# A planner's order against a written one: the first MLP's second product in a fused attention and MLP kernel

## The chip, the cores and the metric

The kernel runs on one core of one Trainium2 chip. The metric is the device time of one execution in microseconds (us), of which the median of several runs is given. The core's engines are TensorE (PE; its weight loads are listed as PEld), VectorE (DVE), ScalarE (ACT), GpSimd (POOL, hardly used here) and SyncE (SP), which issues nearly all DMA transfers here; SPq is its queue in the profile.

## The reference

```python
x = attention(q, k, v, phi)          # 8 batches, 8 heads, 576 positions, 64 wide -> 4608 tokens of 512
h = x @ w_in;   r = np.maximum(h, 0.0);   g = s * (r * r) + b
x = (g @ w_out).astype(np.float32)                        # first MLP, 512 -> 2048 -> 512
h = x @ w_in2;  r = np.maximum(h, 0.0);   g = r * r
return (g @ w_out2).astype(np.float32)                    # second MLP, the same sizes, no s and b
```

The weights come as 64-bit floats; the kernel narrows them to 32 bits itself with integer operations.

## The kernel before, in words

There are four stages. The first computes the attention, folded into the first MLP's first product (`hidden`), and stores the ReLU'd rows `r` to DRAM (`rd`). The second, the subject here, squares them and multiplies them with `w_out` into `x1d` (tiles `ya`, `yb`, `yc`). The third is the second MLP's first product (`pa`, `pb`, `pc`), the fourth its second (`qa`, `qb`, `qc`).

Each of the three products is done by Strassen's scheme in Winograd's form: two by two quadrants, seven products in place of eight. The sums of quadrants of the weights are prepared ahead (`combos`, and for `w_in2` `prepare_in`), those of the data on the way. Each fp32 operand is split in two halves for the fast matmul format: ACT copies the operand to it, DVE subtracts the copy and so makes the rest; that pair is a *cast*. Three matmuls (`split3`) then make one product.

The second stage has six blocks of 768 tokens (`NBLK1`). For each block the four quadrants `b11`, `b12`, `b22`, `b21` are loaded in two halves each (`quad`; the room of a quad is reused by a later one: `rc_room`, and the pool `z` for `b22` and `b21`), squared on ACT (`square`), and subtracted from each other on DVE (`less`). A product `e` (0 to 6) goes in four parts, each with a cast of 128x768 (`cast`, five buffers in the pool `c_p`) and 12 matmuls. A block has 28 parts, the stage 168; a part is called a slot below, numbered through. At the end of each product two `yo` operations take it out of PSUM: ACT at e 0, 1, 2, 6, DVE at 3, 4, 5. From e 3 on each sends its result to `x1d` through SP.

Beside this, `prepare_in` makes the seven weight forms of `w_in2` for the third stage, in eight units `u` of 128 columns: load two raw halves (`wt`), narrow each in four steps (one on ACT, three on DVE, `wx`), four sums on DVE (`ws`), then seven casts of 128x256 (`wc`, two buffers), each with its own store (`wid`). It is a generator: the loop of the second stage takes a step of it once, twice or not at all per part.

What sets the order: the wrapper `Written` puts each instruction behind the one written before it on the same engine as long as `Written.held` is true. That holds in the first stage, whose lists (`TABLE`) give each step a slot of its loop (256 slots of six matmuls). At its end it becomes false, and from there the tile framework's planner chooses the order on each engine from its own costs. Then `behind()` only keeps an instruction behind the last output operation on its engine. In the second stage `ready1.upto` writes everything for part g + 4 ahead of the matmuls of part g, in the order of `block_ready`. In `BEGUN` slots of the first stage the first two squares and four casts of block 0 are already done.

Near the end of the first stage the lists also load quads of block 0: `TABLE["qd"]` gives the slots 225, 227, 240 and 244 for `b11` (two halves) and `b12` (two halves). `b22` is loaded after the stage. The room of `b12`'s second half is the one that held `w_out` units 6 and 7 until their sums are made (`wo1_combos`, tiles `w` and `ws`).

Of the kernel before, what the change touches and what calls it, by code (L numbers as in the profile page):

```python
# [8 lines left out]
F32 = mybir.dt.float32  # L9
# [8 lines left out]


# [35 lines left out]
def memory_attention_then_two_relu2_mlps(  # L55
# [22 lines left out]
    nc = tc.nc  # L78
# [154 lines left out]
    def prepare_in(pool):  # L233


        def load(u, i):
            src = w_in2.rearrange("(d p) (h f) -> d p h f", p=P, h=2)[:, :, :, u * P:u * P + P]
            raw = pool.tile([P, 1, 512], I64, tag="t", name="wt")
            for d in range(2):
                sp.dma_start(raw[:, 0, d * 2 * P:d * 2 * P + 2 * P].rearrange("p (h c) -> p h c", h=2), src[2 * i + d])  # L240
            return raw

        t = load(0, 0)
        for u in range(NU):
            yield from (None,) * (3 if u == 0 else 1)
            x = wst.tile([P, 2, 512], I32, tag="x", name="wx")
            for i in range(2):
                for step, _ in enumerate(narrow(t, None, x[:, i:i + 1])):
                    if step == 0:
                        yield  # L250
                if i == 0:
                    t = load(u, 1)
                    yield from (None,) * 3
                elif u + 1 < NU:
                    t = load(u + 1, 0)
            yield
            a11, a12, a21, a22 = of_in(x.bitcast(F32))
            sums_ = wst.tile([P, 4, 2, P], F32, tag="x", name="ws")
            s1, s2, s4, s3 = [sums_[:, i] for i in range(4)]
            for out, in0, in1, op in ((s1, a21, a22, ALU.add), (s2, s1, a11, ALU.subtract),  # L260
                                      (s3, a11, a21, ALU.subtract), (s4, a12, s2, ALU.subtract)):
                with behind():
                    dve.tensor_tensor(out=out, in0=in0, in1=in1, op=op)
            yield
            for e, of in enumerate((a11, s1, s2, s4, s3, a12, a22)):
                w = pool.tile([P, 2, 2, P], F32R, tag="wc", name="wc", bufs=2)
                with behind():
                    act.copy(w[:, 0], of)
                    dve.tensor_tensor(out=w[:, 1], in0=of, in1=w[:, 0], op=ALU.subtract)
                sp.dma_start(wid[u][:, e], w.bitcast(F32))  # L270
                yield
                if e in (1, 4):
                    yield
# [362 lines left out]
    def block_ready(n):  # L636
        items = []

        def put(k, go, *args):
            items.append((k, lambda: go(*args)))  # L640

        def less(out, in0, in1):
            out, in0, in1 = [quads[x] for x in (out, in0, in1)]
            with behind():
                dve.tensor_tensor(out=out, in0=in0, in1=in1, op=ALU.subtract)

        def square(t):
            t = quads[t]
            with behind():
                act.activation(t, t, AF.Square)  # L650

        def cast(e, part, t):
            c = c_p.tile([P, UQ, 2, TP], F32R, tag="c", name="rcast")
            src = quads[t][:, part % 2 * UQ:(part % 2 + 1) * UQ]
            with behind():
                act.copy(c[:, :, 0, :], src)
                dve.tensor_tensor(out=c[:, :, 1, :], in0=src, in1=c[:, :, 0, :], op=ALU.subtract)
            cast1[n, e, part] = c

        for e in range(7):  # L660
            for half in range(2):
                b11, b12, b22, b21 = [(n, name, half) for name in ("b11", "b12", "b22", "b21")]
                if e in (0, 1, 2, 5):
                    put(None, square, (b11, b12, b22, None, None, b21)[e])
                if e in (1, 2, 6):
                    put(None, less, *{1: (b11, b12, b11), 2: (b11, b22, b11), 6: (b21, b21, b11)}[e])
                if e == 6:
                    put(None, quad, n + 1, "b12", half)
                for part in (2 * half, 2 * half + 1):
                    put(4 * e + part, cast, e, part, (b11, b11, b11, b22, b12, b21, b21)[e])  # L670
                if e == 3:
                    put(None, less, b12, b22, b12)
                    put(None, quad, *b21)
                if e == 4:
                    put(None, *((quad, n + 1, "b11", half) if n + 1 < NBLK1 else (x_first, half)))
                if e == 6:
                    put(None, quad, n + 1, "b22", half)
        return items

    ready1 = Ready(NBLK1, block_ready)  # L680


# [55 lines left out]
    for at_, (name, half) in zip(TABLE["qd"], (("b11", 0), ("b11", 1), ("b12", 0), ("b12", 1))):  # L738
        on(at_, quad, 0, name, half)
# [6 lines left out]
    for slot in range(SB * B):  # L746
        b, h = divmod(slot, SB)
        f, half = divmod(h, 2)
        if h == 0 and b == B - 2:
            kpart.close()  # L750
            wpools.append(ctx.enter_context(tc.tile_pool(name="wa", bufs=1)))
            turns.append((in_turn([wo1_combos(u) for u in range(NA)]), 1))
        for go, args in events.pop(slot, []):
            go(*args)
        if h == 0 and b == B - 1:
            lpart.close()
            wpools.append(ctx.enter_context(tc.tile_pool(name="wb", bufs=1)))
# [10 lines left out]
        if slot == BEGUN[0]:  # L768
            begun = block_ready(0)
            ready1.items = lambda n: begun if n == 0 else block_ready(n)  # L770
        for _ in range(BEGUN.count(slot)):
            begun.pop(0)[1]()
    assert not events
    Written.held = False
# [50 lines left out]

    for n in range(NBLK1):
        banks, outs = {}, {}
        if n == NBLK1 - 1:
            for _ in win:
                pass  # L830
            w64x.close()
            xpools[1] = ctx.enter_context(tc.tile_pool(name="xc0", bufs=1))
        for e in range(7):
            key = "acacaba"[e]
# [4 lines left out]
            for part in range(4):  # L839
                ahead = 28 * n + 4 * e + part + 4  # L840
                ready1.upto(ahead // 28, ahead % 28)
                for _ in range((1, 0, 1, 2, 1, 1, 1)[e]):
                    next(win, None)
                for d in range(2):
                    for u in range(UQ):
                        w = weight("one", part * UQ + u, e)
                        for i, (wi, xi) in enumerate(split3):
                            nc.tensor.matmul(to[d], lhsT=w[:, wi, d], rhs=cast1[n, e, part][:, u, xi],  # L848
                                             start=(start and part == 0 and u == 0 and i == 0),
                                             stop=(part == 3 and u == UQ - 1 and i == 2), skip_group_check=True)  # L850
            which, high = ((0, 0), (1, 1), (0, 1), (0, 1), (1, 1), (0, 0), (1, 0))[e]
            key = which, high
            if key not in outs:
                outs[key] = o1_p.tile([P, 2, TP], F32, tag="o", name="yo")
                for d in range(2):
                    st["act"] = nc.scalar.activation(outs[key][:, d], to[d], AF.Identity,
                                                     scale=s_sb[:, 0:1], bias=wsum[:, 2 * which + d:2 * which + d + 1])
            else:
                for d in range(2):
                    o = outs[key][:, d]  # L860
                    st["dve"] = nc.vector.scalar_tensor_tensor(out=o, in0=to[d], scalar=s_sb[:, 0:1], in1=o,
                                                               op0=ALU.mult, op1=ALU.add)
            if e > 2:
                t0 = n * TB + high * TP
                nc.sync.dma_start(x1d[t0 // XG][:, 2 * which:2 * which + 2, t0 % XG:t0 % XG + TP], outs[key])
# [194 lines left out]
```

## Time and profile before

| | |
|---|---|
| median of 3 runs | 1449.47 us (1446.84 to 1450.83) |
| the profiled execution | 1449.36 us, span 1447.6 us |
| mean granted clock of TensorE | 0.996 |
| PE busy | 1402.8 us, 97% of the span |
| DVE busy | 1073.6 us, 74% |
| ACT busy | 796.2 us, 55% |

All other times stand in the rows below and are microseconds from the span's start. Durations of neighbouring instructions on one engine overlap a little, so a merged row (x2, x48) is shorter than the sum of its members.

### The profile page before, as it was taken

What the parts mean: (1) busy time and instruction counts of PE and PEld (TensorE: products, weight loads), DVE (VectorE), ACT (ScalarE), POOL (GpSimd) and SP (SyncE); (2) the same over time, 40 slices, a digit from 0 to 9 for tenths busy, and PEclk for the clock granted to TensorE, in tenths of its full rate; (3) what the DMA queues carried; (4) which work ended last, traced back from release to release, by engine and by line L of the source; (5) the groups of instructions that cost most, each with busy time, mean ns of one, the idle gap of its engine ahead of it and who ended that gap; (6) DMA issues with size and microseconds to landing.
All of it is one profiled execution on the core that took longest, in us unless ns stands there. A gap on an engine that the chain in (4) does not pass through costs nothing.

```text
span 1447.6 us, 28018 instructions
## 1 busy us (share of the span) xinstructions
PE 1402.8 (97%) x11360; PEld 1347.9 (93%) x11360; DVE 1073.6 (74%) x1550; ACT 796.2 (55%) x1403; POOL 1.2 (0%) x8
## 2 busy tenths in 40 slices
PE   4899999998999999999999999999999999999998
PEld 2688888888999999999999999999999999999998
DVE  6767787666798988888758687786657776777775
ACT  3555666677767767677445455454434444444443
POOL 0000000000000000000000000000000000000000
PEclk9999999999999999999999999999999999999999
DMA  9979888536585584854895664756797334433441
GB/s 299 302 240 290 281 276 283 186 121 217 158 272 183 181 266 148 270 163 164 303 369 193 234 232 168 283 174 259 266 356 262 112 122 146 146 125 111 129 146 30
DMA packets 211473, 306.44 MB, mean 212 GB/s; under 512 B 48656, under 2 KB 163344, under 8 KB 203792
## 3 DMA queue, kind: packets, MB, share of 16 engines
q1 hardware_dynamic: 211184, 304.40, 62.8%
q8 instruction: 89, 1.46, 0.4%
q14 instruction: 40, 0.33, 0.1%
q10 hardware_dynamic: 160, 0.26, 0.0%
HBM read 180.88 MB, written 123.73 MB: 210 GB/s over the span
## 4 chain that ended last, share of the span: by engine, by line
PE 71%; DVE 11%; DMA 9%; ACT 4%; issue 3%; SPq 1%; ACTq 0%; DVEq 0%
PE qa L143 14%; PE pa L141 13%; PE hps L143 13%; PE qc L143 7%; PE pc L141 7%; PE qb L143 4%; PE ya L848 3%; PE pb L141 3%; DVE rcast L141 3%; DMA wid<-wc 3%; PE vps L143 2%; DMA r<-rd 2%; DMA wt<-in_moe_w_in_dram 2%; DVE r L141 2%; PE sp L143 1%
## 5 line engine op out<-in xcount | busy, mean ns | idle before, releaser
L143 PEld LDWEIGHTS hps<-pt,vp 128*128 128x128 f32 x1536 | 208.2, 188 | 37.6 <-issue 18.3
L143 PE MATMUL hps<-pt,vp 128*128 128x288 f32 x1536 | 233.2, 303 | 5.1 <-ACT r L143 2.3
L143 ACT CAST gc<-h 128x1024 fp32r<-128x1024 f32 x119 | 123.3, 1049 | 172.2 <-DVE h L143 171.7
L143 PE MATMUL qa<-w,gc 128*128 128x256 f32 x1728 | 216.7, 283 | 1.1 <-DVE gc L143 0.8
L143 PEld LDWEIGHTS qa<-w,gc 128*128 128x128 f32 x1728 | 211.4, 192 | 1.5 <-DVE gc L143 1.0
L848 PE MATMUL ya<-rcast,w 128*128 128x384 f32 x1152 | 206.2, 338 | 6.3 <-DVE rcast L141 3.8
L143 DVE TENSOR_TENSOR gc<-h,gc 128x1024 fp32r<-128x1024 f32 x119 | 145.6, 1224 | 87.8 <-ACT gc L143 87.7
L848 PEld LDWEIGHTS ya<-rcast,w 128*128 128x128 f32 x1152 | 201.2, 189 | 8.5 <-DVE rcast L141 5.4
L141 PE MATMUL pa<-xc,w 128*128 128x384 f32 x1104 | 204.2, 337 | 0.0
L141 PEld LDWEIGHTS pa<-xc,w 128*128 128x128 f32 x1104 | 192.9, 188 | 0.7 <-DVE gr L141 0.4
L143 ACT ACTIVATE r<-hps 128x288 f32<-128x288 f32 x256 | 104.5, 417 | 66.9 <-PE hps L143 50.1
L143 PE MATMUL qc<-w,gc 128*128 128x256 f32 x864 | 109.5, 283 | 0.0
L848 PE MATMUL yc<-rcast,w 128*128 128x384 f32 x576 | 104.6, 340 | 4.6 <-DVE rcast L141 4.0
L848 PEld LDWEIGHTS yc<-rcast,w 128*128 128x128 f32 x576 | 101.4, 191 | 6.1 <-DVE rcast L141 5.1
L143 PEld LDWEIGHTS qc<-w,gc 128*128 128x128 f32 x864 | 106.3, 192 | 0.0
L141 PE MATMUL pc<-xc,w 128*128 128x384 f32 x552 | 104.0, 336 | 0.0
L141 DVE TENSOR_TENSOR rcast<-r,rcast 128x768 fp32r<-128x768 f32 x92 | 84.3, 953 | 18.0 <-ACT rcast L141 17.9
L141 PEld LDWEIGHTS pc<-xc,w 128*128 128x128 f32 x552 | 96.6, 188 | 0.3 <-DVE xc L822 0.3
L141 ACT CAST rcast<-r 128x768 fp32r<-128x768 f32 x92 | 73.5, 832 | 12.5 <-PE ya L848 5.9
L141 ACT ACTIVATE gr<-pa 128x384 f32<-128x384 f32 x46 | 22.6, 492 | 101.1 <-PE pa L141 101.1
L141 ACT CAST rcast<-rz 128x768 fp32r<-128x768 f32 x72 | 58.7, 834 | 32.4 <-DVE rz L141 15.2
L141 DVE SCALAR_TENSOR_TENSOR gr<-gr 128x384 f32<-128x384 f32 x138 | 73.7, 553 | 1.9
(277 smaller groups left out, 1857.4 us busy)
## 6 DMA issues: line engine op xcount, KB each, us to landing
rd<-r SPq DMA_DIRECT2D x128, 288.0 KB, 4.0
gd<-gr SPq DMA_DIRECT2D x96, 384.0 KB, 3.6
h<-gd SPq DMA_DIRECT2D x34, 1024.0 KB, 5.4
wt<-in_moe_w_out_dram SPq DMA_DIRECT2D x16, 1024.0 KB, 6.8
wid<-wc SPq DMA_DIRECT2D x56, 256.0 KB, 3.8
r<-rd SPq DMA_DIRECT2D x16, 768.0 KB, 5.4
rz<-rd SPq DMA_DIRECT2D x16, 768.0 KB, 6.6
kv<-in_k_dram SPq DMA_DIRECT2D x24, 384.0 KB, 5.3
```

The lines of the kernel that those rows point to most:

```text
L141: return go(*args, **kwargs)
L143: self.last = go(*args, **kwargs)
L848: nc.tensor.matmul(to[d], lhsT=w[:, wi, d], rhs=cast1[n, e, part][:, u, xi], start=(start and part == 0 and u == 0 and i == 0), stop=(part ...
```

## The change

In the second stage `Written.held` stays true on all four engine wrappers: PE, ACT, DVE and SP. `block_steps` gives every square, subtraction, cast and load a slot, by the offsets of `BLK`; within a slot casts come first, then squares, subtractions, loads. Block 0's first eight slots have their own list (`FIRST`). `prepare_in` becomes single operations with a slot each (`WIN`, cut below): `n` is one narrowing step of a half, `s` two of the four sums, `p` a cast of a pair of forms. The casts go by pairs (128x512, the seventh alone), so there are four copies, four subtractions and five stores per unit. The pairs live in the same two tags as the raw loads (`t0`, `t1`), while before there were one buffer for raw loads and two for `wc`. The second half of `b12` of block 0 is loaded after the first stage. The pool `z` is opened ahead of `o1`. The preparation now ends in slot 152; before, what was left of it was done at the start of the last block.

```diff
+WIN = ((0, "load", 0, 0), (0, "load", 0, 1), (5, "n", 0, 0, 0), (8, "n", 0, 0, 1), (9, "n", 0, 0, 2), (9, "n", 0, 0, 3), (9, "n", 0, 1, 0), (11,
...
+       3), (90, "s", 4, 0), (90, "s", 4, 1), (91, "p", 4, 0), (92, "p", 4, 1), (95, "p", 4, 2), (96, "p", 4, 3), (97, "load", 5, 0), (98, "load",
+       5, 1), (101, "n", 5, 0, 0), (102, "n", 5, 0, 1), (102, "n", 5, 0, 2), (102, "n", 5, 0, 3), (102, "n", 5, 1, 0), (103, "n", 5, 1, 1), (103,
+       "n", 5, 1, 2), (106, "n", 5, 1, 3), (107, "s", 5, 0), (109, "s", 5, 1), (111, "p", 5, 0), (113, "p", 5, 1), (115, "p", 5, 2), (117, "load",
...
+       2), (139, "n", 7, 0, 3), (140, "n", 7, 1, 0), (141, "n", 7, 1, 1), (141, "n", 7, 1, 2), (143, "n", 7, 1, 3), (146, "s", 7, 0), (146, "s", 7,
+       1), (147, "p", 7, 0), (148, "p", 7, 1), (151, "p", 7, 2), (152, "p", 7, 3))
+BEGIN1 = (("sq", 0, "b11"), ("cast", 0, 0), ("cast", 0, 1), ("sq", 1, "b11"), ("cast", 0, 2), ("cast", 0, 3))
+FIRST = ((0, "sq", 0, "b12"), (0, "less", 0, "b11", "b12", "b11"), (0, "cast", 1, 0), (1, "cast", 1, 1), (1, "sq", 1, "b12"),
+         (1, "less", 1, "b11", "b12", "b11"), (2, "cast", 1, 2), (3, "cast", 1, 3), (3, "sq", 0, "b22"), (3, "less", 0, "b11", "b22", "b11"),
+         (4, "cast", 2, 0), (5, "cast", 2, 1), (5, "sq", 1, "b22"), (5, "less", 1, "b11", "b22", "b11"), (6, "cast", 2, 2), (7, "cast", 2, 3))
+BLK = {"sq": {0: -5, 1: -8, 2: -8, 5: -5}, "less": {1: -6, 2: -6, 4: -6, 6: -6}, "cast": -4, "b21": 10, "b11": 14, "b12": 18, "b22": 22}
...
+        def pair(u, k):
+            x = xs[u].bitcast(F32).rearrange("p i f -> p (i f)").rearrange("p (e k h c) -> p h e k c", e=2, k=2, h=2)
+            of = (ts["s", u][:, 0:2], ts["s", u][:, 2:4], x[:, 0], x[:, 1, 1:2])[k]
+            m = 2 if k < 3 else 1
+            w = pool.tile([P, 2, 2, 2, P], F32R, tag=f"t{k % 2}", name="wc")[:, :m]
+            act.copy(w[:, :, 0], of)
+            dve.tensor_tensor(out=w[:, :, 1], in0=of, in1=w[:, :, 0], op=ALU.subtract)
+            for i in range(1) if k != 2 else range(2):
+                e, j = ((1, slice(0, 2)), (3, slice(0, 2)), (5 * i, slice(i, i + 1)), (6, slice(0, 1)))[k]
+                sp.dma_start(wid[u][:, e:e + (2 if k < 2 else 1)], w[:, j].bitcast(F32))
...
+        for n in range(NBLK1):
+            for e in range(7):
+                g = 28 * n + 4 * e
+                for half in range(2):
+                    h = 2 * half
+                    name = {0: "b11", 1: "b12", 2: "b22", 5: "b21"}.get(e)
+                    if name and g + h + BLK["sq"][e] >= 0:
+                        on(g + h + BLK["sq"][e], 2, square, n, half, name)
...
+                    for part in (h, h + 1):
+                        if g + part + BLK["cast"] >= 0:
+                            on(g + part + BLK["cast"], 1, cast, n, e, part)
...
-    for at_, (name, half) in zip(TABLE["qd"], (("b11", 0), ("b11", 1), ("b12", 0), ("b12", 1))):
+    for at_, (name, half) in zip(TABLE["qd"], (("b11", 0), ("b11", 1), ("b12", 0))):
...
-    Written.held = False
...
+    z_pool.append(bpart.enter_context(tc.tile_pool(name="z", bufs=1, side="right")))
     o1_p = bpart.enter_context(tc.tile_pool(name="o1", bufs=3, side="right"))
-    z_pool.append(bpart.enter_context(tc.tile_pool(name="z", bufs=1, side="right")))
...
-    for half in range(2):
-        quad(0, "b22", half)
+    for name, half in (("b12", 1), ("b22", 0), ("b22", 1)):
+        quad(0, name, half)
...
             for part in range(4):
-                ahead = 28 * n + 4 * e + part + 4
-                ready1.upto(ahead // 28, ahead % 28)
-                for _ in range((1, 0, 1, 2, 1, 1, 1)[e]):
-                    next(win, None)
+                for go, *args in parts.pop(28 * n + 4 * e + part, []) + win.pop(28 * n + 4 * e + part, []):
+                    go(*args)
...
+    assert not parts
+    Written.held = False
```

## Rows read from the trace of the kernel before

**Rows 1.** Waits of PE, second stage: waiter, releaser, us in total, times, longest.

```profile
PE yc L848 <- DVE rcast L141: 4.0, 4, 1.9
PE ya L848 <- DVE rcast L141: 3.8, 4, 1.6
...
PE yc L848 <- ACT rcast L141: 0.6, 1, 0.6
PE ya L848 <- ACT rcast L141: 0.2, 1, 0.2
```

**Rows 2.** Timeline, PE: start, duration, what, count, idle before it and releaser.

```profile
362.72 10.17 PE L848 MATMUL ya<-rcast,w 128*128 128x384 f32 x48 [2.28 <-ACT r L143]
...
598.47 7.74 PE L848 MATMUL ya<-rcast,w 128*128 128x384 f32 x43 [1.58 <-DVE rcast L141]
...
718.81 8.48 PE L848 MATMUL ya<-rcast,w 128*128 128x384 f32 x48
...
727.13 2.27 PE L141 MATMUL pa<-xc,w 128*128 128x384 f32 x12
...
1079.08 3.04 PE L143 MATMUL qa<-w,gc 128*128 128x256 f32 x24
```

**Rows 3.** Windows: stretch, length, engines' busy us, granted clock, DMA share, GB/s.

```profile
363.60:367.00 3.40, 3.40 (x13) 3.40 (x12) 2.93 (x2) 2.95 (x4) 0.00 (x0) 0.50 0.29 114
...
554.80:558.10 3.30, 3.30 (x12) 3.30 (x11) 2.98 (x4) 3.30 (x4) 0.00 (x0) 0.50 0.39 146
...
483.40:544.00 60.60, 59.89 (x344) 59.26 (x344) 52.99 (x70) 41.21 (x55) 0.00 (x0) 1.00 0.64 206
```

**Rows 4.** Timeline, one stall: ACT's hold and PE's wait after it.

```profile
544.71 0.41 ACT L141 CAST wc<-ws 128x256 fp32r<-128x256 f32 x1 [4.88 <-DMA wid<-wc]
...
553.43 6.88 PE L848 MATMUL yc<-rcast,w 128*128 128x384 f32 x29 [1.86 <-DVE rcast L141]
```

**Rows 5.** Timeline of SP's queue and of ACT where the second stage starts.

```profile
347.29 3.63 SPq L143 DMA_DIRECT2D rd<-r  x2
356.22 0.92 SPq L143 DMA_DIRECT2D r<-rd  x2
357.20 5.82 SPq L143 DMA_DIRECT2D rd<-r  x6
...
359.71 0.88 ACT L143 CAST rcast<-r 128x768 fp32r<-128x768 f32 x1
361.96 0.71 ACT L143 ACTIVATE r<-hps 128x288 f32<-128x288 f32 x2 [1.37 <-DMA rd<-r]
362.55 2.87 ACT L141 ACTIVATE r<-r 128x1536 f32<-128x1536 f32 x2
```

**Rows 6.** Waits of SP's queue from 340 to 375 us.

```profile
SPq L143 <- DVE w L143: 5.2, 1, 5.2
```

**Rows 7.** Groups by line and shape, second stage: busy us, mean ns of one.

```profile
L141 DVE TENSOR_TENSOR rcast<-r,rcast 128x768 fp32r<-128x768 f32 x92 | 84.3, 953 | 18.0 <-ACT rcast L141 17.9
L141 ACT CAST rcast<-r 128x768 fp32r<-128x768 f32 x92 | 73.5, 832 | 12.5 <-PE ya L848 5.9 <-DVE r L141 5.6
...
L141 DVE TENSOR_TENSOR r<-rz,r 128x1536 f32<-128x1536 f32 x24 | 41.6, 1753 | 4.4 <-ACT rz L141 4.4
...
L141 DVE SCALAR_TENSOR_TENSOR wx<-wt,wx 128x512 int32<-128x512 int32 x32 | 22.0, 687 | 0.4
...
L141 DVE TENSOR_TENSOR wc<-ws,wc 128x256 fp32r<-128x256 f32 x32 | 13.4, 420 | 13.9 <-ACT wc L141 13.7
...
L861 DVE SCALAR_TENSOR_TENSOR yo<-yc,s_sb,yo 128x384 f32<-128x384 f32 x12 | 7.2, 611 | 0.0
```

**Rows 8.** DMA issues from 350 to 727 us: count, KB each, median us to landing.

```profile
wid<-wc SPq DMA_DIRECT2D x56, 256.0 KB, 3.8
...
r<-rd SPq DMA_DIRECT2D x14, 384.0 KB, 4.8
```

More of the change, by code (lines that the diff above doesn't have):

```diff
@@ L233, in prepare_in @@
     def prepare_in(pool):
+        ts, xs, steps = {}, {}, {}
         def load(u, i):
             src = w_in2.rearrange("(d p) (h f) -> d p h f", p=P, h=2)[:, :, :, u * P:u * P + P]
-            raw = pool.tile([P, 1, 512], I64, tag="t", name="wt")
+            ts[u, i] = pool.tile([P, 1, 512], I64, tag=f"t{i}", name="wt")
             for d in range(2):
-                sp.dma_start(raw[:, 0, d * 2 * P:d * 2 * P + 2 * P].rearrange("p (h c) -> p h c", h=2), src[2 * i + d])
-            return raw
@@ L243, in prepare_in @@
[L243 to L250, printed above, removed]
-                if i == 0:
[L252 to L273, printed above, removed]
@@ L275, in load_out @@
+        for at_, go, *args in WIN:
+            steps.setdefault(at_, []).append((dict(n=narrow_half, s=add_up, p=pair, load=load)[go], *args))
+        return steps
     def load_out(w, u):
@@ L634, in x_first @@
         first_x.append(t)
[L636 to L660, printed above, removed]
-            for half in range(2):
[L662 to L678, printed above, removed]
@@ L680, in memory_attention_then_two_relu2_mlps, with lessen, square, cast @@
-    ready1 = Ready(NBLK1, block_ready)
+    def lessen(n, half, out, in0, in1):
+        out, in0, in1 = [quads[n, x, half] for x in (out, in0, in1)]
+        dve.tensor_tensor(out=out, in0=in0, in1=in1, op=ALU.subtract)
+    def square(n, half, name):
+        t = quads[n, name, half]
+        act.activation(t, t, AF.Square)
+    def cast(n, e, part):
+        c = c_p.tile([P, UQ, 2, TP], F32R, tag="c", name="rcast")
+        src = quads[n, ("b11", "b11", "b11", "b22", "b12", "b21", "b21")[e], part // 2][:, part % 2 * UQ:(part % 2 + 1) * UQ]
+        act.copy(c[:, :, 0, :], src)
+        dve.tensor_tensor(out=c[:, :, 1, :], in0=src, in1=c[:, :, 0, :], op=ALU.subtract)
+        cast1[n, e, part] = c
@@ new lines, in block_steps, with on @@
+    def block_steps():
+        steps = {}
+        def on(g, rank, go, n, *args):
+            steps.setdefault(g, []).append((rank, len(steps.get(g, [])), go, n, *args))
+        for n in range(NBLK1):
[6 more added lines that the diff above has]
+                        on(g + h + BLK["sq"][e], 2, square, n, half, name)
+                    if e in (1, 2, 4, 6) and g + h + BLK["less"][e] >= 0:
+                        on(g + h + BLK["less"][e], 3, lessen, n, half, *{1: ("b11", "b12", "b11"), 2: ("b11", "b22", "b11"),
+                                                                      4: ("b12", "b22", "b12"), 6: ("b21", "b21", "b11")}[e])
+                    for part in (h, h + 1):
+                        if g + part + BLK["cast"] >= 0:
+                            on(g + part + BLK["cast"], 1, cast, n, e, part)
+            for half in range(2):
+                g = 28 * n + 2 * half
+                on(g + BLK["b21"], 5, quad, n, "b21", half)
+                if n + 1 < NBLK1:
+                    for name in ("b11", "b12", "b22"):
+                        on(g + BLK[name], 5, quad, n + 1, name, half)
+                else:
+                    on(g + BLK["b11"], 5, lambda n, half: x_first(half), n, half)
+        for g in range(8):
+            steps[g] = [x for x in steps[g] if x[3] or not (x[2] is cast and x[4] in (1, 2) or x[2] in (lessen, square))]
+        for g, go, *args in FIRST:
+            on(g, 1, dict(sq=square, less=lessen, cast=cast)[go], 0, *args)
+        return {g: [x[2:] for x in sorted(todo, key=lambda x: x[:2])] for g, todo in steps.items()}
@@ L767, in memory_attention_then_two_relu2_mlps @@
                     turns.remove(turn)
[L768 to L772, printed above, removed]
+        for go, *args in [x for a, x in zip(BEGUN, BEGIN1) if a == slot]:
+            dict(sq=square, cast=cast)[go](0, *args)
     assert not events
-    Written.held = False
     for turn, _ in turns:
@@ L824, in split_x @@
         return sums(b11, b12, b21, b22, cast)
+    parts = block_steps()
     for n in range(NBLK1):
         banks, outs = {}, {}
[L828 to L832, printed above, removed]
         for e in range(7):
+            if (n, e) == (NBLK1 - 1, 5):
+                assert not win
+                w64x.close()
+                xpools[1] = ctx.enter_context(tc.tile_pool(name="xc0", bufs=1))
             key = "acacaba"[e]
@@ L864, in memory_attention_then_two_relu2_mlps @@
                 t0 = n * TB + high * TP
[L865 removed]
+                sp.dma_start(x1d[t0 // XG][:, 2 * which:2 * which + 2, t0 % XG:t0 % XG + TP], outs[key])
             if n == NBLK1 - 1 and e == 3:
```

20 lines of the change are left out of this document (17 added, 3 removed), and 12 rows, old and new, of the table WIN.

## The prediction

> **What bounds the kernel now.** I read the waits of TensorE (PE) first. In the stage that the change touches, the first MLP's second product, PE stands idle for products that are not cast yet: 4.0 + 3.8 us for VectorE's (DVE's) half of a cast and 0.6 + 0.2 us for ScalarE's (ACT's), 8.6 us in ten waits [rows 1]. Idle time understates the loss, so the timeline of PE comes second. At full pace 48 matmuls take 727.13 - 718.81 = 8.32 us, 0.1733 us each [rows 2]. The stage has 2016 matmuls (6 blocks x 7 products x 48), so 349.4 us at that pace. It begins at 362.72 and the next stage's first matmul is at 727.13 [rows 2]: 364.4 us, **15.0 us over its floor**.
>
> [...]
>
> Fourth, why the casts are late. DVE is busy 52.99 us in a block of 60.6 [rows 3]: much, but not full. The planner's order is what fails. ACT stood 4.88 us at a small `wc` copy until a `wid` store had freed its buffer; less than 9 us later PE waited 1.86 us for a cast [rows 4].
>
> Outside this stage there is little to gain here. The next one runs from 727.13 to 1079.08 [rows 2], 352.0 us for 2016 matmuls as well, only 2.5 over the same floor.
>
> **The change part by part.**
>
> *The written order of blocks.* A slot is one part of a product, 12 matmuls, 2.08 us. The code casts part g+4 at slot g, four slots (8.32 us) ahead. A cast takes 0.83 us on ACT and 0.95 on DVE [rows 7], so 6.5 us of slack remain for everything that delays it. What can use that slack up is DVE work that bunches. I went through the lists slot by slot with the durations of rows 7; the worst place is slots 102 to 104. Slot 102: a cast 0.95, a quad subtraction 1.75, narrowing steps 0.42 (priced by the 128x256 `wc` row) + 2 x 0.69 = 4.50. Slot 103: 0.95 + 0.42 + 0.69 + two `yo` sums 1.22 = 3.28. Slot 104: 0.95 + 1.75 = 2.70. Together 10.5 us in 6.2 us of slots: DVE is 4.2 us behind, 2.3 us inside the slack. Everywhere else it is less. ACT never falls more than 3 us behind. [...]
>
> *Squares and loads earlier.* A square is now due 5 to 6 slots (10.4 to 12.5 us) after the load of its quad, except for the first block. A load piece lands 4.8 us after issue [rows 8], and the subtraction that frees its room comes up to 4 us into its slot. That leaves 2 us or more, and a miss costs ACT's slack before it costs PE.
>
> *w_in2's preparation.* Per unit, seven copies, seven subtractions and seven stores of 128x256 become four copies, four subtractions and five stores. DVE: 56 x 0.42 = 23.5 us [rows 7] become 8 x 0.42 and 24 of 128x512, priced at 0.69 by the 128x512 `wx` row: 19.9, so 3.6 us less; ACT saves about as much. Neither is the bound: counted as 0 on the path. The copies share two buffers with the raw loads, so each third pair waits for the first one's store, and each next load for the third's. A `wid` store of 256 KB lands in 3.8 us [rows 8]; one of 512 KB I take at 4.8 (the 384 KB row), between 3.8 and twice that. The pairs are at least four slots apart (8.3 us); a subtraction up to 2 us into the next slot, 0.4 for the issue and 4.8 make 9.3 us: ACT may stand about 1 us at a third pair. Under its slack: 0 on the path.
>
> *The moved load.* Before, the second half of `b12` stood on SP's queue in the stage ahead of this one, and held it. SP issued nothing between 350.9 and 356.22 [rows 5], waiting for DVE to be done with `w` [rows 6]. Six `rd` stores came only after it, from 357.20 [rows 5]. ACT then waited 1.37 us for an `r` tile to be stored before its last two ReLUs [rows 5], and PE for those ReLUs [rows 2]. Now the two pieces come after the last store. ACT's last cast ends at 359.71 + 0.88 = 360.59, the ReLUs take 0.71 [rows 5], so the stage begins at 361.3: **1.4 us gained**. [...]
>
> What becomes late instead: with one more `rd` store ahead, these pieces are issued by 362.6 and land at 367.4 (4.8 us, rows 8). Square 1.44 (half of 2.87, rows 5) to 368.9, subtraction 1.75 to 370.6, cast 1.8 to 372.4; its product is due at 361.3 + 6 x 2.08 = 373.8. The next cast's DVE half ends at 373.4. Then b22's two halves go the same serial way: 1.75 + 1.8 gives 376.9 (due at 377.9), the part after it 377.9, and again 1.75 + 1.8 gives 381.4 (due at 382.1). The slack is 0.7 us at its smallest. The cost lies between 0 and 3 us (a landing 2 us later, with a restart and a clock stretch); I take 1.
>
> *Pools, and the end.* `z` moved ahead of `o1`, so b22's load need not wait for the last `r` stores: not on the path. The last unit's preparation now ends in slot 152 instead of before the last block, 16 slots (33 us) ahead of the next stage; `wid`'s later loads wait for weight buffers, as before. After the loop the planner orders again, from another state. Bounds: nothing, or a second time the 2.5 us that the next stage loses now; I take 1.
>
> **Sum**, against the profiled execution's 1449.36 us: -15.0 - 1.4 + 1 (first block) + 1 (one stall left over in the other five) + 1 (later stages) = -13.4, so **1436.0 us**. The median of the runs shown is 1449.47, the same within 0.1, so the number stands for it.
>
> **The rivals.**
>
> *Partly.* The planner's bunching goes, but two or three of the ten stalls per stage come back as waits of ACT for loads and stores, and the first block pays its 3 us. Half of the 15.0 goes: 1449.4 - 7.5 + 1 = 1443. For it: ACT's longest hold now is such a wait [rows 4]. Against: each needs more than 6.5 us, and that hold was 4.88.
>
> *No effect.* The lead of four parts was in the code before too (`ahead`), so the stalls might be bursts of DVE work that no order cures: 1449. Against: 52.99 of 58.2 us at full pace is 91%, and the lists spread it.
>
> *Slower: head of line on SP and ACT.* SP must issue in the written order now, and a load of the next unit stands there until the third pair's store has landed; the quads of b22 stand behind it (slots 77 to 80 and 133 to 136, and at the start of five other units), ACT's square waits for them, and every cast behind the square waits too. The trace shows the first link at 350.9 to 356.2 [rows 5, 6]. It decides from the point at which ACT is held over 6.5 us. [...] Against: in the case I worked (unit 4) the load is free by slot 80, b22 lands by slot 84, where the square is due, and a hold of one or two us costs nothing.
> [...]
>
> **How the numbers follow.** About 0.3% (4.3 us) is what a measurement of this kernel can tell from no change. Forecast 70%, on its own 1432.5 to 1440: the floor is 1449.4 - 16.4 = 1433, and the runs shown spread by 2 us. Partly 14%, no effect 8%, slower 8%. Faster 0.84, same 0.08, slower 0.08. The range is 1432.5 to 1445: it takes in the forecast and the partial case.
>
> **What would show it.** PE's waits in this stage fall from 8.6 us to 2 or less, the stage takes 350 to 353 us, no stretch at half clock remains in it, it begins near 361.3, and ACT's waits for `wid` stores become few and under 5 us. Wrong would be: PE waiting at slots 6 to 10 of the first block by several us, a hole on SP ahead of a b22 load with PE idle some four slots later, or a next stage longer than 355 us.

## The result, and the profile after

The changed kernel takes **1436.93 us** (median of 5 runs, 1434.08 to 1439.19), the kernel before, run beside it, 1449.07 (5 runs, 1445.22 to 1450.83). The ratio is 0.9917, 95% interval 0.9895 to 0.9939: 12.1 us or 0.8% faster. The prediction was 1436.0. The profiled execution took 1436.93 us as well, with a span of 1435.1 against 1447.6.

The page after, busy us of each engine, and the chain that ended last:

```profile
PE 1401.4 (98%) x11360; PEld 1348.7 (94%) x11360; DVE 1073.5 (75%) x1526; ACT 791.0 (55%) x1379; POOL 1.2 (0%) x8
...
PE 91%; DVE 4%; DMA 2%; ACT 2%; issue 1%; SPq 0%; ACTq 0%
```

PE is busy for 98% of the span and 91% of the chain: little is left to take from its waits.

The waits of PE in the second stage after (waiter, releaser, us in total, times, longest). This one line is all that stands there, where [rows 1] had 8.6 us in ten waits:

```profile
PE ya L168 <- ACT r L168: 0.8, 1, 0.8
```

It is the wait at the start of the stage, as the timeline after shows (start, duration, what, count, idle before and its releaser):

```profile
349.27 14.23 SPq L168 DMA_DIRECT2D rd<-r  x8
...
362.39 0.76 ACT L168 ACTIVATE r<-hps 128x288 f32<-128x288 f32 x2
363.21 8.61 PE L168 MATMUL ya<-rcast,w 128*128 128x384 f32 x48 [0.81 <-ACT r L168]
363.90 0.98 SPq L168 DMA_DIRECT2D r<-rd  x2
368.94 1.49 ACT L168 ACTIVATE r<-r 128x1536 f32<-128x1536 f32 x1 [1.02 <-DMA r<-rd]
...
712.78 2.27 PE L166 MATMUL pa<-xc,w 128*128 128x384 f32 x12
```

The eight `rd` stores run through without the hole of [rows 5], the two load pieces come after them at 363.90, ACT's last ReLUs wait for no store, and PE stood 0.81 us instead of 2.28 [rows 2]. The stage takes 712.78 - 363.21 = 349.57 us, which is the floor of 349.4.

Windows after (stretch, length, busy us and instructions of PE, weight load, DVE, ACT and POOL, granted clock, DMA share, GB/s): the first block and one in the middle.

```profile
363.20:421.60 58.40, 58.39 (x337) 58.39 (x338) 48.41 (x57) 41.17 (x49) 0.00 (x0) 1.00 0.66 211
...
538.10:596.30 58.20, 58.20 (x338) 58.20 (x336) 52.81 (x66) 40.34 (x51) 0.00 (x0) 1.00 0.60 199
```

These blocks take 58.2 to 58.4 us where the one in [rows 3] took 60.6. DVE works as long as before (52.81 against 52.99): the work is not less, it stands at better places. The clock is at 1.00 throughout.

**Where the time went, profile against profile.** Stages are read from the timelines of PE, here and for the runs below: the second from its first `ya` matmul to the first `pa` matmul, the third from there to the first `qa` matmul, and the gap from the start of the last `hps` matmul to the first `ya`.

| us | before | after | difference |
|---|---|---|---|
| first stage, to its last `hps` matmul | 360.15 | 362.10 | +1.95 |
| gap to the first `ya` matmul | 2.57 | 1.11 | -1.46 |
| second stage | 364.41 | 349.57 | -14.84 |
| third stage | 351.95 | 353.72 | +1.77 |
| rest | 368.49 | 368.62 | +0.13 |

The sum is -12.45 (-12.5 by the spans). The +1.95 of the first stage lies ahead of every changed instruction. The traces are level up to 45 us, and then the one after has a stretch at half clock that the one before has not. The window of each, after and then before:

```profile
55.40:58.80 3.40, 3.40 (x44) 3.12 (x47) 1.36 (x3) 2.32 (x7) 0.00 (x0) 0.50 0.58 234
```

```profile
55.40:58.80 3.40, 3.40 (x154) 3.24 (x157) 1.38 (x3) 3.40 (x8) 0.00 (x0) 1.00 0.85 326
```

44 matmuls against 154 in the same time. In the experiments below that issue the same instructions there, the last `hps` matmul starts anywhere from 358.1 to 362.2: at 360.1 or earlier in the four without a stretch at half clock between 52 and 66 us, at 360.9 or later in those with one. So this term is spread between executions and not the change.

### The profile page after: what moved, and what is told of

Same layout as the page of the kernel before. It is cut to its first block, busy times and chain, and to the rows that moved or that the text cites. A ratio compares the mean times of both kernels' runs of the same rounds, so it can differ in the third digit from the quotient of the medians.

```text
span 1435.1 us, 27884 instructions
## 1 busy us (share of the span) xinstructions
PE 1401.4 (98%) x11360; PEld 1348.7 (94%) x11360; DVE 1073.5 (75%) x1526; ACT 791.0 (55%) x1379; POOL 1.2 (0%) x8
## 3 DMA queue, kind: packets, MB, share of 16 engines
q8 instruction: 89, 1.46, 0.4%
## 4 chain that ended last, share of the span: by engine, by line
PE 91%; DVE 4%; DMA 2%; ACT 2%; issue 1%; SPq 0%; ACTq 0%
PE qa L168 14%; PE ya L168 14%; PE pa L166 13%; PE hps L168 12%; PE qc L168 7%; PE yc L168 7%; PE pc L166 6%; PE qb L168 4%; PE yb L168 3%; PE pb L166 3%; PE vps L168 2%; PE sp L168 1%; PE kvs L168 1%; PE qps L168 1%; DVE wx L168 1%
## 5 line engine op out<-in xcount | busy, mean ns | idle before, releaser
L168 PE MATMUL ya<-rcast,w 128*128 128x384 f32 x1152 | 202.9, 336 | 0.8 <-ACT r L168 0.8
L168 DVE TENSOR_TENSOR rcast<-r,rcast 128x768 fp32r<-128x768 f32 x96 | 90.7, 954 | 20.4 <-ACT rcast L168 19.6
L168 ACT CAST rcast<-r 128x768 fp32r<-128x768 f32 x96 | 78.1, 833 | 36.8 <-DVE r L168 28.4
L168 DVE TENSOR_TENSOR rcast<-rz,rcast 128x768 fp32r<-128x768 f32 x72 | 68.0, 953 | 14.7 <-ACT rcast L168 14.2
L168 ACT CAST rcast<-rz 128x768 fp32r<-128x768 f32 x72 | 58.4, 835 | 36.5 <-DVE rz L168 23.5
```

What stands on the lines that cost most here:

```text
L168: self.last = go(*args, **kwargs)
```

## The experiments

All are timed against the kernel before on the same chip. Ratios have their 95% interval. The stages come from each run's own trace.

| run | median us | ratio | gap | second stage | third stage |
|---|---|---|---|---|---|
| e1 planner orders | 1443.59 | 0.9964 (0.9951 to 0.9976) | 1.10 | 355.10 | 353.85 |
| e2 no pairs | 1437.55 | 0.9916 (0.9902 to 0.9931) | 1.10 | 349.54 | 353.20 |
| e4 before, with pairs | 1449.18 | 0.9990 (0.9980 to 0.9999) | 2.67 | 362.52 | 353.31 |
| e5 SP not held | 1434.08 | 0.9898 (0.9882 to 0.9915) | 1.11 | 349.55 | 351.72 |
| e3 load moved back | 1438.83 | 0.9931 (0.9908 to 0.9954) | 2.51 | 351.13 | 353.27 |
| e6 three slots ahead | 1438.93 | 0.9928 (0.9906 to 0.9950) | 1.10 | 350.93 | 353.57 |
| e7 two slots ahead | 1448.12 | 0.9987 (0.9976 to 0.9999) | 1.10 | 361.07 | 353.68 |
| e8 short holds | 1443.67 | 0.9950 (0.9932 to 0.9969) | 1.10 | 355.41 | 353.51 |
| e9 long holds | 1464.83 | 1.0116 (1.0100 to 1.0133) | 1.11 | 379.01 | 353.69 |
| e10 order held longer | 1435.78 | 0.9913 (0.9899 to 0.9926) | 1.10 | 349.89 | 353.90 |
| e11 squares written late | 1467.35 | 1.0122 (1.0098 to 1.0147) | 1.10 | 379.84 | 354.46 |
| e12 earlier `w` loads | 1441.54 | 0.9942 (0.9920 to 0.9964) | 1.10 | 349.66 | 360.99 |

**e1: the lists of the change, but the planner's order.**

```
     assert not parts
+    Written.held = False
```

> The changed kernel, but Written.held becomes false where it did before, ahead of the second stage; lists, pairs, pools and the moved load stay. Theory (the order on ACT and DVE is what removes the stalls): the planner bunches DVE work again, PE waits 4 us or more for casts, the second stage (first ya matmul to first pa matmul) takes 355 to 364 us against 349.6 with the written order and 364.4 before, total 1442 to 1451. Rival (the lists write everything early enough, whoever orders it): stage 350 to 351 us, total within 2 us of 1437.

The stage takes 355.10 us, 5.5 more than in the change, at the lower edge of what the theory gave. But it is 9.3 under the stage before, so the order is not the whole gain. PE's waits:

```profile
PE ya L166 <- DVE rcast L166: 1.8, 4, 0.5
PE yc L166 <- DVE rcast L166: 1.5, 2, 1.1
```

3.3 us in six waits where [rows 1] had 8.6 in ten; the theory gave 4 or more.

**e2: the written order, each form of `w_in2` by itself again.**

```
-            act.copy(w[:, :, 0], of)
-            dve.tensor_tensor(out=w[:, :, 1], in0=of, in1=w[:, :, 0], op=ALU.subtract)
-            for i in range(1) if k != 2 else range(2):
-                ...
+            for j in range(m):
+                act.copy(w[:, j, 0], of[:, j])
+                dve.tensor_tensor(out=w[:, j, 1], in0=of[:, j], in1=w[:, j, 0], op=ALU.subtract)
+                sp.dma_start(wid[u][:, ((1, 2), (3, 4), (0, 5), (6,))[k][j]], w[:, j].bitcast(F32))
```

> The changed kernel with each pair of w_in2's forms done as single copies, subtractions and stores of 128x256, in the same slots, rooms and written order: 56 of each in place of 32, 32 and 40. Theory: DVE gets 3.6 us more work and ACT about as much, spread over 152 slots, inside the slack: stage 349.5 to 351 us, no PE wait over 1 us. Rival (fewer and larger operations did it): PE waits return, stage 354 us or more, total 1442 or more.

349.54 against 349.57: the pairs are worth nothing in the written order.

**e4: the kernel before with the pairs alone**, two buffers shared with the raw loads. The next unit's first raw load goes out behind the third pair in place of ahead of the casts. The line shown is the one of the buffers.

```
-                w = pool.tile([P, 2, 2, P], F32R, tag="wc", name="wc", bufs=2)
+                w = pool.tile([P, 2, 2, 2, P], F32R, tag=f"t{k % 2}", name="wc")[:, :m]
```

> The kernel before with w_in2's preparation in pairs and in the two rooms of the changed kernel, everything still in the planner's order and b12 where it was. Theory: stage 358 to 366 us, PE waits for casts 5 to 10 us, total 1442 to 1451. Rival (the pairs did it: no more ACT holds for a wc buffer): stage 350 to 354 us, total 1435 to 1440.

The ratio is 0.999: next to nothing. The stage falls by 1.9 us to 362.52. This run decides on the cause that the prediction gave for the stalls, ACT held by a `wid` store [rows 4]. ACT's waits for such stores in this stage, before and then in e4:

```profile
ACT wc L141 <- DMA wid<-wc: 26.4, 15, 4.9
```

```profile
ACT wc L141 <- DMA wid<-wc: 5.6, 6, 1.7
```

And yet PE still waits for casts in e4:

```profile
PE yc L852 <- DVE rcast L141: 2.4, 2, 2.2
PE ya L852 <- DVE rcast L141: 2.2, 3, 0.8
...
PE yc L852 <- ACT rcast L141: 1.2, 1, 1.2
```

20.8 us of holds less brought 1.9 us of the stage. So the `wid` stores alone were not the main cause. But e4 does not clear ACT's holds as such: its largest stall, 1.19 + 2.17 us of the 6.0 that PE waits for casts, comes after ACT stood 4.63 us for a raw load, with two squares, two subtractions and the cast in between:

```profile
606.73 0.67 ACT L141 ACTIVATE wx<-wt 128x512 f32<-128x512 f32 x1 [4.63 <-DMA wt<-in_moe_w_in_dram]
...
612.81 0.44 PE L852 MATMUL yc<-rcast,w 128*128 128x384 f32 x1 [1.19 <-ACT rcast L141]
...
615.42 2.93 PE L852 MATMUL yc<-rcast,w 128*128 128x384 f32 x8 [2.17 <-DVE rcast L141]
```

All of ACT's waits for raw loads (`wt`) in this stage are 11.0 us in e4 and 6.2 before: one hold went and another came.

**e11: the written order, with squares and quad subtractions written right ahead of the casts that need them**, instead of one to four slots (squares) and two slots (subtractions) earlier.

```
-BLK = {"sq": {0: -5, 1: -8, 2: -8, 5: -5}, "less": {1: -6, 2: -6, 4: -6, 6: -6}, "cast": -4, ..., "b12": 18, ...}
+BLK = {"sq": {0: -4, 1: -4, 2: -4, 5: -4}, "less": {1: -4, 2: -4, 4: -6, 6: -4}, "cast": -4, ..., "b12": 20, ...}
```

> The changed kernel, all in written order, but with squares and subtractions written right ahead of the casts that need them (a square, a subtraction and a cast in one slot, four slots ahead of the product), as the kernel before writes them, in place of one to four slots earlier; the subtraction for product 4 stays where it was. With e1_planner this makes a square of four: late and planner's order (before, 364.4 us), early and planner's (e1_planner, 355.1), early and written (the change, 349.6), late and written (this). Theory A (what counts is how early squares and subtractions are written): the stage loses most of what lies between before and e1_planner, 355 to 362 us. Theory B (the planner's interleaving makes the stalls, and any written order with the casts four slots ahead is free of them): 349.5 to 351.5 us.

379.84 us: 30.3 more than the change and 15.4 more than the kernel before, far over the ranges of both theories, and the whole is 1.2% slower than before. The longest of PE's waits, and one stall in the timeline:

```profile
PE ya L168 <- ACT rcast L168: 8.7, 7, 2.4
PE ya L168 <- DVE rcast L168: 5.4, 11, 0.6
```

```profile
467.65 0.66 ACT L168 ACTIVATE wx<-wt 128x512 f32<-128x512 f32 x1 [4.64 <-DMA wt<-in_moe_w_in_dram]
...
469.07 0.96 DVE L168 TENSOR_TENSOR rcast<-rz,rcast 128x768 fp32r<-128x768 f32 x1 [5.07 <-ACT rcast L168]
...
472.79 1.75 DVE L168 TENSOR_TENSOR rz<-rz,r 128x1536 f32<-128x1536 f32 x1
...
474.63 1.56 ACT L168 CAST rcast<-rz 128x768 fp32r<-128x768 f32 x2 [4.88 <-DVE rz L168]
...
475.51 0.44 PE L168 MATMUL ya<-rcast,w 128*128 128x384 f32 x1 [1.30 <-ACT rcast L168]
```

ACT stood 4.64 us for a raw load and so copied the cast behind it late. DVE stood 5.07 us for that copy and so subtracted late, ACT stood again 4.88 us for that subtraction, and PE 1.30 us for the next cast: three steps that hand work from one engine to the other and back, with a lead of four slots. All of e11's stalls for casts stand in products 1, 2 and 6 of a block, the ones whose casts need a square or a quad subtraction first. After, the same waits of ACT exist:

```profile
ACT rcast L168 <- DVE r L168: 28.4, 19, 3.3
ACT rcast L168 <- DVE rz L168: 23.5, 9, 4.3
ACT wx L168 <- DMA wt<-in_moe_w_in_dram: 15.3, 11, 3.2
```

but there the casts are reached early enough that none of them gets to PE. In e11's trace the cast behind the held narrowing step ran only after the 4.64 us, at 468.22.

**e6 and e7: every step of the blocks one and two slots later**, casts three and two slots ahead; the list of block 0's first slots (`FIRST`) and the steps of `w_in2` stay. The diff is e6's; in e7 the values are -2, 12, 16, 20 and 24, and squares and subtractions move by the same one or two slots.

```
-BLK = {..., "cast": -4, "b21": 10, "b11": 14, "b12": 18, "b22": 22}
+BLK = {..., "cast": -3, "b21": 11, "b11": 15, "b12": 19, "b22": 23}
```

> The changed kernel with every step of the blocks (casts, squares, subtractions, loads) one slot later, so a cast is written 3 slots ahead of its product instead of 4; w_in2's steps stay in their slots. Slack by the prediction's sum: 6.24 less 1.8 for the cast, 4.4 us, against a worst DVE backlog of 4.2 by mean durations. Theory: stage 349.5 to 352 us. Rival (the slack is already used up at four slots by waits that the sum left out): 354 us or more.

> The same two slots later: a cast is written 2 slots ahead. Slack 4.16 - 1.8 = 2.3 us against a backlog that goes over 2.3 us in about six places by mean durations (up to 4.2). Theory: PE waits 0.5 to 2 us in four to eight places, 3 to 10 us in all, stage 353 to 362 us. Rival (the lead is not what covers DVE; its work is spread well enough by itself): stage 350 to 351 us.

The first slot costs 1.4 us (350.93), the second 10.1 more (361.07), both inside the theories' ranges. Most of PE's waits in e7:

```profile
PE ya L168 <- DVE rcast L168: 5.4, 10, 0.8
```

But the agreement is not the sum's doing: the lead of four slots has less to spare than the prediction worked out. Take for each part, in the timelines after, the time from the end of its cast on DVE to its first matmul. This margin is under one slot, 2.08 us, in 18 of the 168 parts; the least are 0.37 us (part 10, in the first block) and 0.46 us (part 109, whose cast is written in slot 105). The second stands right behind the prediction's worst place, slots 102 to 104:

```profile
577.11 0.66 ACT L168 ACTIVATE wx<-wt 128x512 f32<-128x512 f32 x1 [0.64 <-DMA wt<-in_moe_w_in_dram]
...
578.52 0.96 DVE L168 TENSOR_TENSOR rcast<-rz,rcast 128x768 fp32r<-128x768 f32 x1 [3.08 <-ACT rcast L168]
...
588.65 2.00 DVE L168 TENSOR_TENSOR rcast<-rz,rcast 128x768 fp32r<-128x768 f32 x2
...
587.98 5.19 PE L168 MATMUL ya<-rcast,w 128*128 128x384 f32 x29
```

DVE begins the work of slot 102 at 578.52, 3.08 us idle, because ACT's copy came late, behind a square and two short waits for loads. It needs 10.1 us for the three slots, where the sum gave 10.5, but it is through only at 588.65. PE began slot 105 at 363.21 + 105 x 2.08 = 581.6, so DVE is 7 us behind and not 4.2. The first cast of the row at 588.65 is done at 589.6; its part begins 12 matmuls after 587.98, at 590.06. In e6, PE's two stalls for casts stand elsewhere, at parts 143 and 145.

**e8 and e9: the pairs of a unit written close together**, so that a third pair stands for the first one's store (shown for unit 0; the first added line is e8's, the second e9's).

```
-(17, "p", 0, 0), (19, "p", 0, 1), (23, "p", 0, 2), (24, "p", 0, 3)
+(17, "p", 0, 0), (19, "p", 0, 1), (19, "p", 0, 2), (20, "p", 0, 3)
+(17, "p", 0, 0), (17, "p", 0, 1), (17, "p", 0, 2), (17, "p", 0, 3)
```

> The changed kernel with the third pair of each unit written in the slot of the second and the fourth one slot after, so ACT comes to the third pair's copy while the first one's store is under way. Theory: ACT is held 3 to 6 us once in each of 8 units, under the 6.5 us at which PE begins to lose, so the stage stays at 349.5 to 352 us. Rival (head of line: what stands behind a held ACT is late at once): 1 us or more per unit, stage 357 us or more.

> The changed kernel with all four pairs of a unit written in the slot of the first: ACT's third copy comes right behind the second, and the first one's store has still to be subtracted, issued and landed. Theory: ACT is held 6 to 9 us per unit, at and over the 6.5 us from which PE loses; PE waits 0 to 3 us per unit, some half-clock stretches, stage 355 to 375 us. Rival (no hold of this size matters, since the casts come out of the backlog in time): stage under 352 us.

ACT's waits for `wid` stores, e8 and then e9:

```profile
ACT wc L151 <- DMA wid<-wc: 24.2, 11, 4.2
```

```profile
ACT wc L151 <- DMA wid<-wc: 32.8, 16, 3.9
```

No hold is over 4.2 us, and yet e8 loses 5.8 us and e9 29.4. Neither theory held: e8 lies between its theory and its rival, and e9's holds are shorter and its stage longer than expected. One place in e8:

```profile
562.23 0.62 ACT L151 CAST wc<-wx 128x512 fp32r<-128x512 f32 x1 [2.01 <-DMA wid<-wc]
...
564.64 2.54 PE L151 MATMUL yc<-rcast,w 128*128 128x384 f32 x13 [0.55 <-DVE rcast L151]
```

A hold of 2.01 us is enough for PE to stand 0.55 us within 3 us: the 6.5 us are not there to spend. The part is number 97, whose cast has a margin of 3.58 us in the change. ACT came to this unit's first pair about 2 us later than in the change, measured against PE's parts, and the hold came on top. It is not DVE's backlog that was met here: by its timeline DVE itself stood 1.59 us for the held copy. The longest of PE's waits in e9:

```profile
PE yc L151 <- ACT rcast L151: 8.4, 5, 3.1
PE yb L151 <- DVE rcast L151: 3.1, 4, 1.2
```

**e3: the second half of `b12` loaded in the first stage again.**

```
-    for at_, (name, half) in zip(TABLE["qd"], (("b11", 0), ("b11", 1), ("b12", 0))):
+    for at_, (name, half) in zip(TABLE["qd"], (("b11", 0), ("b11", 1), ("b12", 0), ("b12", 1))):
...
-    for name, half in (("b12", 1), ("b22", 0), ("b22", 1)):
+    for name, half in (("b22", 0), ("b22", 1)):
```

> The changed kernel with the second half of b12 loaded in slot 244 of the first stage again. Theory: SP stands about 5 us behind that load, the last r stores come late, ACT waits 1 to 2 us for an r tile before the last ReLUs, and the gap from the last hps matmul to the first ya matmul is about 2.6 us (it is 2.6 before and 1.1 with the change); a half-clock stretch of 3.4 us may follow, 1.5 us; the rest of the stage is unchanged, 349.6 us without that stretch. Total 1.4 to 3 us more than with the change. Rival (the gap differs from run to run for another reason): gap near 1.1 us.

```profile
357.51 0.94 SPq L168 DMA_DIRECT2D r<-rd  x2
358.50 5.74 SPq L168 DMA_DIRECT2D rd<-r  x6
...
363.94 8.27 PE L168 MATMUL ya<-rcast,w 128*128 128x384 f32 x37 [2.22 <-ACT r L168]
```

```profile
364.00:367.40 3.40, 3.40 (x11) 3.40 (x12) 1.76 (x1) 1.57 (x2) 0.00 (x0) 0.51 0.90 293
```

The timeline and the window show the picture of before again: load, late stores, 2.22 us of idle PE, half clock after it. The gap grows by 1.40 us, the stage by 1.56: 3.0 us for one line. The ratios agree in sign (0.9931 against 0.9917) and are not apart by their intervals; the rows are.

**e5: SP's queue left to the planner in this stage**, ACT and DVE in the written order.

```
-                if not Written.held:
+                if not Written.held or self.free:
...
+    sp.free = True
```

> The changed kernel with SP's issues in the second stage ordered by the planner, PE, ACT and DVE as written. Theory (SP is not what mattered): stage 349.5 to 352 us, PE waits under 2 us, total within 3 us of 1437. Rival (the main queue's order carries the gain, because loads and stores queue up in a bad order otherwise): PE waits of 4 us or more, stage 354 or more.

The stage is the same, 349.55 us: the written order is needed on the two engines, not on the queue. The third stage is back at 351.72. SP's queue in e5 at the end of the stage:

```profile
705.10 1.52 SPq L166 DMA_DIRECT2D w<-wid  x3
709.68 0.37 SPq L166 DMA_DIRECT2D x1d<-yo  x1
710.15 9.01 SPq L166 DMA_DIRECT2D w<-wid  x9
```

Three of the next stage's weight loads go out at 705.10, ahead of the last store. e5 has the lowest median, but its interval overlaps those of the change and of e2: whether it beats the change is open.

**e10 and e12: what the third stage lost.** Of its 1.8 us, 1.5 stand in its first 60 matmuls, the rest near its end. The start, by the timeline after:

```profile
718.12 0.62 PE L166 MATMUL pa<-xc,w 128*128 128x384 f32 x2 [0.69 <-ACT xc L847]
...
722.76 1.29 PE L166 MATMUL pa<-xc,w 128*128 128x384 f32 x6 [0.17 <-DMA w<-wid]
```

e10 holds the written order through the first two units of that stage (first diff), e12 issues four of the `w` loads after the sixth product of the last block and no longer in the list behind the loop (second diff, the addition).

```
-    Written.held = False
...
+                else:
+                    assert not pre
+                    Written.held = False
```

```
+                for u in range(4, 8):
+                    load_unit(wid, "in", u, (0,))
```

> The changed kernel with the written order kept through the first two units of the third stage, whose casts are written two products ahead of their use. The changed kernel loses about 1.6 us there (PE's matmuls late at 715.4, 718.1 and 722.7), the kernel before 0.3. Theory (the planner's order after the loop is what costs it): those waits go to 0.5 us or less, third stage 352.0 to 352.7 us instead of 353.7, total 1 to 1.5 us less than with the change, too little to tell by the times. Rival (the weights' loads are late there, whatever the order): no gain, 353.5 us or more.

> The changed kernel with the first chunks of w_in2's units 4 to 7 loaded after product 5 of the last block, where their rooms are free, instead of after the loop behind the last result's store. Theory (in the written order these loads come late, and with SP left to the planner three loads went out ahead of that store and the third stage took 351.7 us): PE's wait for w goes, third stage 352.5 to 353.3 us against 353.7, the second stage stays at 349.6. Rival (the third stage differs by ACT's and DVE's order at its start alone): 353.5 us or more. By the times it can't be told from the change.

Neither theory held. e10's third stage is 353.90. e12's is 360.99, 7.3 worse; SP's queue and PE's waits there:

```profile
708.14 2.33 SPq L168 DMA_DIRECT2D w<-wid  x4
713.27 11.68 SPq L168 DMA_DIRECT2D w<-wid  x8
```

```profile
PE pa L166 <- DMA w<-wid: 4.8, 1, 4.8
```

The chunk that PE needs first left SP at 713.27, 1.4 us after the stage's start, and so no later than in the change (714.09, 1.3 us after it). But now four loads of 1 MB were on their way ahead of it, and PE stood 4.8 us for it; the clock stood at half from 724.4 to 731.2. e12 moved the wrong loads.

The kept traces show more than the totals of the stage do. By its 96th matmul the third stage is behind full pace by 0.4 us before, in e4 and in e5, and by 1.9 us in the change. e1 and e4, with totals of 353.85 and 353.31, lose their time elsewhere: e1 1.3 us at one wait for a `w` load, e4 after its 1000th matmul. e5, which differs from the change in SP's order alone, has the start of before. Two of the three loads at 705.10 in e5 are second chunks (768 KB), among them the one that `pb` needs. In the change they stand behind the last store, from 714.09 on. In e5 PE goes on after its first 24 matmuls with two of `pb`, where in the change it took two of `pa`, whose cast was not there yet (718.12 above):

```profile
713.27 0.51 PE L166 MATMUL pb<-xc,w 128*128 128x384 f32 x2
```

So SP's written order at the end of the second stage costs the 1.5 us at this start. That it does so by these two loads is the likely reading; no run moves them alone.

## Why the prediction was right

**The sum.** By terms, forecast and measured: stage to its floor -15.0, -14.84; start of the stage -1.4, -1.46; first block +1, 0; one leftover stall +1, 0; later stages +1, +1.9; and +1.95 in the first stage that no term had. -13.4 against -12.45. The two cautious +1 that did not come are made up for by the first stage's clock stretch, which is luck.

**Start of the stage.** Right in mechanism and size, and e3 shows it alone: the load piece on SP held the stores, these held ACT's ReLUs, and half clock followed the 2.2 us of idle PE. The stage began at 363.21 instead of 361.3 because of the first stage.

**First block.** Expected late by at most a hair, with 0.7 us of slack at the smallest, and priced at 1, in a range of 0 to 3 us whose top counts a restart and a clock stretch. No run shows what a restart alone costs; here neither came, as PE has no wait for a cast in the block and its granted clock is 1.00 from 363.20 to 421.60. The casts in question in the timeline after, two in each row, of 0.95 us (the first of each row counts here):

```profile
373.18 1.83 DVE L168 TENSOR_TENSOR rcast<-r,rcast 128x768 fp32r<-128x768 f32 x2 [0.96 <-ACT rcast L168]
...
382.81 1.83 DVE L168 TENSOR_TENSOR rcast<-r,rcast 128x768 fp32r<-128x768 f32 x2 [0.96 <-ACT rcast L168]
```

Counted from the start of the stage, 363.21, the square of `b12`'s second half came at +5.7 us (forecast +6.1), the cast on it was done at +10.9 (forecast +11.1), and the last one of b22 at +20.5 (forecast +20.1), its product due at +20.8. No wait and no cost, with 0.3 to 0.4 us to spare: the chain of ACT and DVE could be added up by hand to half a microsecond.

**The slack of the written order.** Right in its outcome, too small in its size. The sum has DVE 4.2 us behind at its worst place, 2.3 us inside the slack, and then says: "Everywhere else it is less." Measured, DVE is 7 us behind there and 0.46 us are left. The sum counts DVE's own work and leaves out that DVE also waits for ACT, 3.08 us ahead of this place, while ACT waits for loads. That no stall came of it was a matter of half a microsecond, which is luck.

**w_in2's preparation.** Counted as 0 on the path: for the pairs, right in the written order (e2). Its raw loads, for which ACT waits 15.3 us in the stage after, are in no term.

**The step that failed: "The planner's order is what fails."** The saving came as forecast, but this step gives it to the order alone, and takes ACT's hold at a `wid` store [rows 4] for the cause. e11 kept the written order and wrote the squares and subtractions late: 15.4 us worse than the planner. e1 kept the early lists and left the order to the planner: 9.3 of 14.8 us. Of these 9.3, up to 1.9 are the pairs (e4) and some 1.6 the moved load (e3). The remaining 5.8, by subtraction, belong to the lists as a whole: squares one to four and subtractions two slots ahead of the cast's own slot, earlier loads, and slots for the steps of `w_in2`. No run takes these apart under the planner. For squares and subtractions speaks where the stalls stand: before, all nine behind the stage's start are in products 1, 2 and 6 of a block (that before 553.43 in product 1, that before 598.47 in product 6), whose casts need a square or a subtraction first, and so are all of e11's.

As for the hold, e4 took away 20.8 us of the 26.4 us at `wid` stores and won 1.9, so these stores are not the cause by themselves. What the stalls shown share is a hold of ACT by some transfer of the preparation: 4.88 us at a store before [rows 4], 4.63 us at a raw load in e4, 4.64 us at one in e11. What stood behind it on ACT, DVE's subtraction and the cast that needs it then came late one after the other. In the change ACT still waits up to 3.2 us for a raw load, without a stall of PE. The prediction had "Squares and loads earlier" as a question of room for loads; in the written order it decides (e11), and without it that order is a loss.

**The rivals.** *Partly* and *no effect* fell with PE's waits at 0.8 us. *Slower, head of line* did not happen, but half of its mechanism is real: e9 holds ACT at its own copies, for 3.9 us at most and two times per unit, and comes to 1464.8 us. The other half, a quad's load stuck on SP and a square late for it, is in no run; ACT waits for a quad only 0.9 us in e9. Its deciding point was wrong: "ACT is held over 6.5 us" counted the whole slack, as if nothing else used it. The margins after go down to 0.46 us, and e8 loses 5.8 us with no hold over 4.2. In the change itself the first link is there, on SP's queue in its waits after:

```profile
SPq L168 <- DMA wid<-wc: 34.9, 14, 6.2
```

and the second is not: ACT waits 1.5 us in all for quads, and for a `wid` store not at all. The pairs of a unit stand far enough apart, which e8 shows to be necessary: with the third and fourth pair two to four slots earlier, 5.8 of the 14.8 us are lost.

## What to carry to other kernels

Before fixing the order on several engines by hand, count the hand-overs between them ahead of each deadline, and write each producer early enough to stand in no queue with its consumer: the same written order won 14.8 us with its squares and subtractions early and lost 15.4 with them late. Slack is spent once: take the backlog from it before asking how long a wait may be, and count into the backlog that each engine also waits for the other. A long wait next to a stall is a suspect, not a cause, until taking it away moves the stall; and where it is taken away, look whether another has come in its place.

## What the runs showed of the hardware

Idle time of PE and the clock: 0.81 us idle at the start of the stage was followed by full clock in the change (1.00 from 363.20 to 421.60), as were 1.58 us in the kernel before [rows 2] (1.00 from 598.50 to 606.00), while 1.86, 2.22 and 2.28 us were followed by a stretch of 3.3 to 3.4 us at half clock [rows 3, e3]. But idle time alone does not tell: in e11 1.40 us before 438.85 were followed by full clock and 1.30 us before 475.51 by half clock (0.50 from 476.5 to 479.8), with one matmul and a second stall of 0.55 us behind both. The second stage of e7, with 13 waits of PE for casts, 6.8 us in all and 0.9 us the longest, had no half clock (mean granted clock of the execution 0.996), while the first stage went to half clock at 55.4 us in one execution (0.50 from 55.40 to 58.80, after) and not in another of the same instructions (1.00 in the same window, before).

Loads in flight and the next one: in e12 the chunk that PE needed, issued as early as in the change but behind four loads of 1 MB, kept PE waiting 4.8 us, where in the change PE waited 0.2 us for `w`.
